# A state-space scan with a gated feed-forward behind it: pair 3 loaded two tokens to a partition and turned by DMA, weights loaded in five groups

## The chip, the cores and the metric

The kernel runs on one core of a Trainium2 chip. The core has five engines with instruction queues of their own: TensorE (PE, with its weight loads PEld) multiplies matrices into PSUM, VectorE (DVE) and ScalarE (ACT) read PSUM and SBUF, GpSimd (POOL) works on SBUF alone, and SyncE (SP) issues DMAs. ACT and POOL issue DMAs too. A DMA that changes the type on its way (the weights here, from fp32 to bf16) is issued by POOL. All DMAs share sixteen DMA engines. An engine runs its own instructions in order, and waits on semaphores for the others.

The metric is device time in microseconds. Thirteen runs of the kernel before have a median of 126.57 us (125.64 to 130.33). The profiled execution took 126.45 us, of which 124.7 us are the profile's span.

## The reference

There are 4 batches of 768 tokens, 8 heads, 32 channels per head and a state of 16. Part one is a linear recurrence with a decay a per token, written by chunks; part two is a feed-forward with a product of two branches:

```python
    for c in range(nc):
        ...
        L = np.exp(cum[:, :, :, None] - cum[:, :, None, :])
        L = L * causal
        CB = np.einsum('bhin,bhjn->bhij', Cc, Bc)
        y_intra = np.einsum('bhij,bhjd->bhid', CB * L, xc)
        y_inter = np.einsum('bhin,bhnd->bhid', Cc, state) * decay_to_i[:, :, :, None]
        y[:, :, sl] = y_intra + y_inter
        state = decay_full[:, :, None, None] * state + np.sum(Bx, axis=2)
...
    gate = np.maximum(x @ w_gate, 0.0)
    val = x @ w_val
    return (gate * val @ w_out).astype(np.float32)
```

In part two x is y laid out as 3072 tokens by 256 channels, and the hidden width is 1536.

## The kernel before

The tokens are cut into twelve **pairs** of 256 tokens (two chunks of 128); three pairs make a batch, so pairs 0 to 2 are batch 0 and pair 3 is the first of batch 1. For the feed-forward two pairs make a **block** of 512 tokens; there are six blocks. While TensorE runs the feed-forward of one block, the pieces of the scan for the next pairs are put between, in an order written out by hand. `in_order` ties every engine to that order, so a late instruction holds back all that stand behind it on its engine.

For each pair C and B (`bcr`) and x (`xr`) are loaded, C is multiplied by the running decay of each token and B by its inverse (`scale_wide`, `scale_bc`), x is cast to bf16 (`cast_x`), and B and C are brought with the state dimension onto the partitions. `G` or `G_wide` forms C times B in four PSUM banks, one for four of sixteen head slots each; ACT copies and DVE evacuate them to `gs`, with the causal mask applied on the way or by POOL behind (`gmask`, `gevac`). `adds` or `sums` forms B times x, from which the state is carried. `inter` adds the state's share to y in PSUM, `D_wide` or `Dm` the share within the chunk; `yevac` writes y, transposed, to `yT`, which the feed-forward reads.

The pairs come in two layouts. Pairs 0 to 2 (`p < NWIDE`) are loaded with two neighbouring tokens to a partition: a piece of 128 bytes for B and C and of 256 for x, 1024 pieces a load, three loads a pair. Pairs 3 to 11 are loaded one chunk at a time, one token to a partition: pieces of 64 and 128 bytes, six loads a pair, each with 1024 pieces again. Pairs 0 to 3 are turned on TensorE (`turn`: four transposes into PSUM, then `tevac` or `copy_B` and `copy_C`). Pairs 4 to 11 (`p >= FIRST`) are scaled by POOL into one of four cleared tiles `tok` and turned by a DMA that transposes (L306, on SP), into `turned`.

The feed-forward: `gv` computes gate and val for 128 of the 1536 hidden channels and all 512 tokens, `gvh` for 256 tokens (u names the half of the block); ACT takes the Relu into r, DVE multiplies by val from PSUM into h. `fout` multiplies h by `wo` for 128 tokens, twelve matmuls; `foevac` writes out. Five PSUM banks are shared by all of these (`bank`).

The order of loads is set by three queues. SP issues the loads of pairs 0 and 1, then, once a DVE memset in the target has run (L84, behind yT of pair 0), C, B and x of pair 2, the six loads of pair 3, and the six each of pairs 4 and 5. Behind them come two stores, the turning of pair 4, the loads of pair 6, the turning of pair 5, the loads of pair 7. POOL issues the weights: wg and wv for hidden slices 0 to 1, then 2 to 5, once `wfac` is there (the copy to `gate`, L718); slices 6 to 11 behind the scaling and casting of pair 1; wo, in one piece, behind a mask of pair 1 (L193). Behind these POOL scales pair 2, builds masks, casts pair 2's x, clears the `tok` tiles, masks pair 2 and scales pair 3 (L315).

Later on POOL scales pairs 4, 5 and 6 in turn (L301, L331), and only behind pair 6 masks the scores of pair 4 (L513).

Of the kernel before, what the change touches and what calls it, by code (L numbers as in the profile page):

```python
# [29 lines left out]
def kernel(  # L30
# [44 lines left out]
    NWIDE = PPB  # L75
# [3 lines left out]
    def load_bc(p, j, *qs):  # L79
        s = st.setdefault(p, {})  # L80
        if "bcr" not in s:
            s["bcr"] = raw.tile([128, NH, 2, 2, N], FP32, tag="bcr", name="bcr")
            if p == 2:
                nc.vector.memset(s["bcr"][0:1, 0, 1, 0, 0:1], 0.0)  # L84
        n = NH // len(qs)
        for i, q in enumerate(qs):
            hs = slice(i * n, (i + 1) * n)
            q.dma_start(
                out=s["bcr"][:, hs, j].rearrange("p h r n -> p h (r n)"),
                in_=(B, C)[j][0, hs, p * 256:(p + 1) * 256, :].rearrange(  # L90
                    "h (p r) n -> p h (r n)", r=2))

    def load_x(p, *qs):
        xr = raw.tile([128, NH, 2, D], FP32, tag="xr", name="xr")
        n = NH // len(qs)
        for i, q in enumerate(qs):
            hs = slice(i * n, (i + 1) * n)
            q.dma_start(out=xr[:, hs].rearrange("p h r d -> p h (r d)"),  # L98
                        in_=x[0, hs, p * 256:(p + 1) * 256, :].rearrange(
                            "h (p r) d -> p h (r d)", r=2))  # L100
        st.setdefault(p, {})["xr"] = xr
# [84 lines left out]
    def weights(f0, f1):  # L186
        fs = slice(f0 * 128, f1 * 128)
        for w, src in ((wg, moe_w_gate), (wv, moe_w_val)):
            nc.gpsimd.dma_start(
                out=w[:, :, fs], in_=src[:, fs].rearrange("(k p) f -> p k f", k=2))  # L190
# [5 lines left out]

    gate = const.tile([1, 2], FP32)
# [36 lines left out]
    def middle():  # L234
        nc.vector.reciprocal(rmid, cp[:, H - 1:H])
        nc.gpsimd.tensor_scalar_mul(pick[:, 0], pairs[:, 0], rmid)

    scaleBC = glob.tile([128, NB, NC, 2, 8], FP32)

    def decay():  # L240

        d = mm.tile([128, HC, 2, NB, 8], FP32, tag="tp", name="dec")
        for k in range(HC):
            nc.tensor.matmul(
                out=d[:, k].rearrange("p w b h -> p (w b h)"),
                lhsT=cp[:, k * 128:(k + 1) * 128],
                rhs=pick.rearrange("p w h -> p (w h)"),
                start=(k == 0), stop=True, skip_group_check=True)
        st["dec"] = d

    def decay_factors():
        d = st["dec"]
        for w in range(2):
            cs = slice(w * HC, (w + 1) * HC)
            nc.scalar.copy(
                out=scaleBC[:, :, cs, 1, :].rearrange("p b k h -> p k b h"), in_=d[:, :, w])
# [11 lines left out]

    def scale_wide(p, j, eng):
        s = st[p]  # L270
        if "bs" not in s:
            s["bs"] = bs = att.tile([128, 4, 128], BF16, tag="bs", name="bs")
            s["tin"] = [[bs[:, 2 * j + r] for r in range(2)] for j in range(2)]
        src = s["bcr"].rearrange("s (t q) j r n -> s j r t q n", t=2)[:, j]
        f = wfac[:, j, :, :, p]
        for t in range(2):
            eng.tensor_tensor(
                out=s["bs"][:, 2 * j:2 * j + 2].rearrange(
                    "s k (q t n) -> s k t q n", q=4, t=2)[:, :, t],
                in0=src[:, :, t],  # L280
                in1=f[:, :, 4 * t:4 * t + 4].to_broadcast([128, 2, 4, N]),
                op=ALU.mult)

    FIRST = 4
    NTOK = 4
    tok = [glob.tile([128, 6, 128], BF16, name="tok%d" % i) for i in range(NTOK)]

    def scale_bc(p, eng):
        b, c0 = p // PPB, 2 * (p % PPB)
        s = st[p]
        if p >= FIRST:
            bs = tok[p % NTOK]
            src = s["bcr"].rearrange("s i j (t q) n -> s j i t q n", t=2)
            f = scaleBC[:, b, c0:c0 + 2].rearrange("s c j h -> s j c h")
            dst = bs.rearrange("s (j i) (q t n) -> s t j i q n", i=2, q=4, t=2)
            for t in range(2):
                for j in range(2):  # L300
                    eng.tensor_tensor(  # L301
                        out=dst[:, t, j * (1 + t)], in0=src[:, j, :, t],
                        in1=f[:, j, :, 4 * t:4 * t + 4].to_broadcast([128, 2, 4, N]),
                        op=ALU.mult)
            turned = att.tile([128, 6, 128], BF16, tag="turned", name="turned", bufs=4)
            nc.sync.dma_start_transpose(out=turned, in_=bs.rearrange("s k c -> s (k c)"))  # L306
            s["B"] = [bs[:, i] for i in range(2)]
            s["BT"] = turned[:, 0:2]
            s["CT"] = turned[:, 2:6].rearrange("s (t i) m -> s t i m", t=2)
            return  # L310
        bs = att.tile([128, 4, 128], BF16, tag="bs", name="bs")
        src = s["bcr"].rearrange("s i j (t q) n -> s (i j) t q n", t=2)
        f = scaleBC[:, b, c0:c0 + 2].rearrange("s c j h -> s (c j) h")
        for t in range(2):
            eng.tensor_tensor(  # L315
                out=bs.rearrange("s k (q t n) -> s k t q n", q=4, t=2)[:, :, t],
                in0=src[:, :, t],
                in1=f[:, :, 4 * t:4 * t + 4].to_broadcast([128, 4, 4, N]),
                op=ALU.mult)
        s["tin"] = [[bs[:, 2 * i + j] for i in range(2)] for j in range(2)]  # L320
        s["B"] = s["tin"][0]
# [67 lines left out]
    def G_wide(p):  # L389
        s = st[p]  # L390
        g = [bank("g%d" % q, (128, 2, 2, 128)) for q in range(4)]
        for r in range(2):
            for i in range(2):
                for q in range(4):
                    rows = slice(32 * q, 32 * q + 32)
                    nc.tensor.matmul(
                        out=g[q][64 * i:64 * i + 64, r],
                        lhsT=s["BT"][rows, r, 64 * i:64 * i + 64], rhs=s["CT"][rows, :, i],
                        start=(r == 0), stop=True, tile_position=(32 * q, 64 * i),
                        skip_group_check=True)  # L400
# [4 lines left out]
    def gmask(p, q, eng, psum=False):  # L405
        s = st[p]
        d = s["gw"][:, q]
        m = wmask.unsqueeze(2).to_broadcast([128, 2, 2, 128])
# [6 lines left out]
    def y_wide(p):  # L415
        s = st[p]
        if "yw" not in s:
            s["yw"] = [mm.tile([128, 512], FP32, tag=t, name=t) for t in ("y", "Aps")]
# [58 lines left out]

    def D_wide(p, qs=(0, 1, 2, 3)):
# [13 lines left out]
    def yevac_wide(p, *engs):  # L492
        s = st[p]
        for i, eng in enumerate(engs):
            dst = yT[:, :, p * 256 + i * 128:p * 256 + (i + 1) * 128]
            (eng.copy if eng is nc.scalar else eng.tensor_copy)(
                out=dst, in_=s["yw"][i][:, 0:256].rearrange("s (t m) -> s t m", t=2))
# [40 lines left out]
    def sums(p):  # L538
# [7 lines left out]
        if c < NC - 2:  # L546
            parts += [(1, s, 0), (1, s, 1)]
        for n, (k, u, i) in enumerate(parts):
            xs = u["x"][i].rearrange("s (t q d) -> s q t d", t=2, q=4)
            for q in range(4):  # L550
                rows = slice(32 * q, 32 * q + 32)
                nc.tensor.matmul(  # L552
                    out=acc["A"][rows, k].rearrange("s (t d) -> s t d", t=2),
                    lhsT=u["B"][i][:, rows], rhs=xs[:, q],
                    start=(c == 0 and n == 0), stop=True, tile_position=(0, 32 * q),
                    skip_group_check=True)
# [92 lines left out]
    def fout(b, ts):  # L649
        if ts % 2 == 0 or b == NBLK - 1:  # L650
# [11 lines left out]
        for f in range(NF):  # L662
# [55 lines left out]
    nc.gpsimd.tensor_copy(gate[:, 0:1], wfac[0:1, 1, 0, 0, 0:1])  # L718
    weights(0, 2)
    weights(2, 6)  # L720
# [11 lines left out]
    cast_x(1, P_)  # L732
# [9 lines left out]
    gcopy(0, 1)  # L742
# [3 lines left out]
    gmask(0, 1, V)  # L746
# [9 lines left out]
    load(2)  # L756
    load(3)
    carry(0, 1)
    weights(6, NF)
    tevac(1, V, A_)  # L760
    pass_on(0, 1)
# [5 lines left out]
    G_wide(1)  # L767
    adds(1)
    decay()
# [7 lines left out]
    gmask(1, 1, P_)  # L777
    weights_out(0, NF)
    gmask(1, 0, V)
    late = [gvh(0, f, 0, True) for f in (1, 2, 3)]  # L780
# [9 lines left out]
    load(4)  # L790
    load(5)
# [7 lines left out]
    for t in range(2):  # L799
        nc.gpsimd.tensor_scalar_mul(smask[:, t], bd, tmask[:, t:t + 1])  # L800
    halves(0, 1, 0, 1, 2, 3, 4, 5)
    gv(0, 6)
    carry(1, 1)
    gv(0, 7)
    pass_on(1, 1)
# [5 lines left out]
    gv(0, 10)  # L811
    gv(0, 11)
    copy_C(2, 1)
    cast_x(2, P_)
    for t in tok:
        nc.gpsimd.memset(t, 0.0)
# [3 lines left out]
    adds(2)  # L820
# [3 lines left out]
    gmask(2, 0, P_)  # L824
    inverse(1, 2)
    gmask(2, 3, V, True)
    gmask(2, 1, V)
    carry(2, 0)
    pass_on(2, 0)
    scale_bc(3, P_)  # L830
    cast_x(3, P_)
    fout(0, 1)
    foevac(0, 1)
# [5 lines left out]
    turn(3)  # L839
    tevac(3, A_, V)  # L840
    fout(0, 3)
    foevac(0, 3)
    G(3)
    sums(3)
    gevac(3)
    states(3)
    halves(1, 0, 0, 1, 2, 3)
    inverse(2, 4)
    inter(3, 1)
    Dm(3)  # L850
    yevac(3, A_)
    halves(1, 0, 4, 5)

    for b in range(1, NBLK):
# [25 lines left out]
        for f in range(n, NF):  # L880
            gv(b, f)
            if b == 1 and at("scale P", 99, 6):
                scale(P, nc.gpsimd, nc.gpsimd)
                load(P + 2)
            if at("scale Q", 9, 6, 4):
# [65 lines left out]
```

## Time and profile before

| what | us |
|---|---|
| median of 13 runs | 126.57 |
| profiled execution | 126.45 |
| its span | 124.7 |
| TensorE busy | 118.1 |
| DVE, ACT, POOL busy | 87.1, 77.0, 47.3 |
| weights and wo, POOL's issue to landing | 4.6 to 10.8 |
| narrow loads of B, C, x on SP, median to landing | 3.7, 3.4, 3.6 |
| a turning DMA on SP, to landing | 3.2 |

In a list of waits a line names the engine and line that idled, what ended the idling, and the sum, the count and the longest, in us. In a timeline a line has the start from the beginning of the span, the duration, the engine (a q behind it is its queue, which issues DMAs), the line, the operation, the tiles as out<-in, the shape and the count of merged instructions; in brackets is the idle time before it and what ended it. The busy table gives busy time, share of the span and number of instructions for each engine.

### The profile page before, as it was taken

To read this page: it belongs to the slowest core of one execution; us is meant where nothing else is said; L and a number is where in the kernel's file an instruction comes from. 1 tells how busy PE (TensorE), PEld (TensorE's weight loads), DVE (VectorE), ACT (ScalarE), POOL (GpSimd) and SP (SyncE) were. 2 spreads that over 40 slices of the span, in tenths; PEclk is the share of its full clock that TensorE was granted. 3 is DMA by queue.
4 is the path that set the end of the run, shared out by engine and by line. 5 is a ranking of instruction groups with operands and counts; after the bars stand their busy time and mean duration, and the time that the engine had idled before them with its cause. 6 is when DMAs were issued, how large, how long until landed. Compare 5 with 4: busy or idle time off the path is not lost.

```text
span 124.7 us, 3580 instructions
## 1 busy us (share of the span) xinstructions
PE 118.1 (95%) x1362; PEld 82.3 (66%) x1368; DVE 87.1 (70%) x192; ACT 77.0 (62%) x169; POOL 47.3 (38%) x106
## 2 busy tenths in 40 slices
PE   6988899997999999999999999999999999999990
PEld 6855585375777468884467874577864677854790
DVE  3795989655499757698853987764997855687510
ACT  0467688844588634787734786726786545876410
POOL 6589622789282309360423810621800033000000
PEclk9999999999999999999999999999999999999999
DMA  3999999977998998699799189991340002200022
GB/s 58 217 173 205 152 222 204 124 89 95 117 119 174 157 120 123 80 251 132 86 114 158 40 180 119 115 158 33 129 104 5 0 0 84 85 4 0 0 84 84
DMA packets 78704, 13.71 MB, mean 110 GB/s; under 512 B 72304, under 2 KB 78688, under 8 KB 78688
## 3 DMA queue, kind: packets, MB, share of 16 engines
q1 hardware_dynamic: 72448, 10.42, 54.2%
q0 software_dynamic: 3184, 2.36, 12.7%
q10 hardware_dynamic: 3056, 0.72, 2.7%
q8 instruction: 10, 0.16, 0.5%
q14 instruction: 6, 0.05, 0.1%
HBM read 11.13 MB, written 3.15 MB: 114 GB/s over the span
## 4 chain that ended last, share of the span: by engine, by line
PE 79%; SPq 11%; DMA 2%; issue 2%; POOL 1%; DVE 1%; ACT 1%; DVEq 0%
PE o L663 22%; PE gv L636 16%; PE val L621 14%; PE gate L618 12%; SPq L116 6%; PE w L180 4%; SPq L117 3%; PE y L593 3%; PE g L505 2%; DMA bcr<-in_C_dram 2%; SPq L98 2%; PE y L582 2%; PE o L657 1%; POOL bs L315 1%; PE A_ps L552 1%
## 5 line engine op out<-in xcount | busy, mean ns | idle before, releaser
L625 DVE TENSOR_TENSOR h<-r,val 128x512 bf16<-128x512 bf16 x44 | 30.3, 688 | 8.2 <-ACT r L624 7.8
L663 PE MATMUL o<-wo,h 128*128 128x256 bf16 x276 | 32.8, 273 | 0.4 <-DMA wo<-in_moe_w_out_dram 0.4
L624 ACT ACTIVATE r<-gate 128x512 bf16<-128x512 f32 x44 | 26.3, 597 | 9.7 <-PE gate L618 9.3
L663 PEld LDWEIGHTS <-h 128*128 128x128 bf16 x276 | 26.0, 98 | 5.5 <-issue 1.5
L621 PE MATMUL val<-yT,wv 128*128 128x512 bf16 x88 | 26.2, 379 | 0.3
L618 PE MATMUL gate<-yT,wg 128*128 128x512 bf16 x82 | 24.9, 379 | 0.0
L642 DVE TENSOR_TENSOR h<-r,gv 128x256 bf16<-128x256 bf16 x56 | 22.5, 418 | 2.5 <-ACT r L639 1.6
L639 ACT ACTIVATE r<-gv 128x256 bf16<-128x256 f32 x56 | 21.4, 384 | 2.3 <-PE gv L636 0.2
L636 PE MATMUL gv<-yT,wv 128*128 128x256 bf16 x112 | 21.4, 273 | 0.5 <-DMA wv<-in_moe_w_val_dram 0.5
L636 PE MATMUL gv<-yT,wg 128*128 128x256 bf16 x112 | 21.5, 273 | 0.2 <-DVE bcr L84 0.2
L530 DVE TENSOR_TENSOR gs<-g,maskUT 128x512 bf16<-128x512 f32 x18 | 11.6, 686 | 12.1 <-issue 5.6
L513 POOL TENSOR_SCALAR_AFFINE_SELECT gs<-gs 128x512 bf16<-128x512 bf16 (+1 forms) x18 | 8.9, 520 | 28.3 <-ACT gs L524 28.3
L301 POOL TENSOR_TENSOR tok<-bcr,scaleBC 128x128 bf16<-128x128 f32 x32 | 12.0, 402 | 20.1 <-DMA bcr<-in_B_dram 19.7
L621 PEld LDWEIGHTS <-wv 128*128 128x128 bf16 x88 | 8.6, 98 | 10.4 <-DMA wv<-in_moe_w_val_dram 0.2
L618 PEld LDWEIGHTS <-wg 128*128 128x128 bf16 x88 | 8.6, 98 | 8.9
L636 PEld LDWEIGHTS <-wv 128*128 128x128 bf16 x112 | 10.9, 98 | 2.0 <-DMA wv<-in_moe_w_val_dram 0.7
L636 PEld LDWEIGHTS <-wg 128*128 128x128 bf16 x112 | 10.2, 98 | 2.2 <-issue 0.4
L524 ACT CAST gs<-g 128x512 bf16<-128x512 f32 x9 | 5.3, 587 | 6.7 <-PE g L505 6.7
L606 ACT CAST yT<-y 128x512 bf16<-128x512 f32 x9 | 5.3, 585 | 5.4 <-PE y L593 2.7
L180 PE MATMUL w<-warm 128*128 128x128 bf16 x49 | 5.9, 296 | 1.1 <-DVE tmask L154 1.1
L180 PEld LDWEIGHTS <-warm 128*128 128x128 bf16 x58 | 5.3, 132 | 1.7 <-DVE tmask L154 1.1
L564 DVE TENSOR_TENSOR Sm<-A_ps,smask 128x256 bf16<-128x256 f32 x15 | 5.7, 416 | 0.0
(115 smaller groups left out, 111.1 us busy)
## 6 DMA issues: line engine op xcount, KB each, us to landing
xr<-in_x_dram SPq DMA_DIRECT2D x19, 128.0 KB, 3.6
out_dram<-ob SPq DMA_DIRECT2D x3, 512.0 KB, 3.3
bcr<-in_C_dram SPq DMA_DIRECT2D x19, 64.0 KB, 3.4
bcr<-in_B_dram SPq DMA_DIRECT2D x19, 64.0 KB, 3.7
out_dram<-ob SPq DMA_DIRECT2D x4, 256.0 KB, 3.0
wo<-in_moe_w_out_dram POOLq DMA_DIRECT2D x1, 768.0 KB, 10.8
xr<-in_x_dram SPq DMA_DIRECT2D x2, 256.0 KB, 9.3
wg<-in_moe_w_gate_dram POOLq DMA_DIRECT2D x1, 384.0 KB, 6.4
```

Source lines behind the costliest of these rows:

```text
L180: nc.tensor.matmul(out=w, lhsT=warm, rhs=rhs, start=True, stop=True)
L301: eng.tensor_tensor(out=dst[:, t, j * (1 + t)], in0=src[:, j, :, t], in1=f[:, j, :, 4 * t:4 * t + 4].to_broadcast([128, 2, 4, N]), op=ALU. ...
L513: nc.gpsimd.affine_select(out=dst, in_=dst, pattern=[[0, n], [1, 128]], compare_op=ALU.is_ge, fill=0.0, base=0, channel_multiplier=-1)
L530: nc.vector.tensor_tensor(out=d[:, q], in0=g[q], in1=m, op=ALU.mult)
L618: nc.tensor.matmul(out=g, lhsT=wg[:, k, fs], rhs=yT[:, k, tk], start=(k == 0), stop=(k == 1))
L621: nc.tensor.matmul(out=v, lhsT=wv[:, k, fs], rhs=yT[:, k, tk], start=(k == 0), stop=(k == 1))
L624: nc.scalar.activation(r, g, AF.Relu)
L625: nc.vector.tensor_tensor(out=fst[b][:, f], in0=r, in1=v, op=ALU.mult)
L636: nc.tensor.matmul(out=gv_[:, j], lhsT=w[:, k, fs], rhs=yT[:, k, tk], start=(k == 0), stop=(k == 1), skip_group_check=True)
L639: nc.scalar.activation(r, gv_[:, 0], AF.Relu)
L642: nc.vector.tensor_tensor(out=fst[b][:, f, u * 256:(u + 1) * 256], in0=r, in1=gv_[:, 1], op=ALU.mult)
L663: nc.tensor.matmul(out=o[:, ts % 2], lhsT=fst[b][:, f, ts * 128:(ts + 1) * 128], rhs=wo[:, f], start=(f == 0), stop=(f == NF - 1), skip_gr ...
```

## The change

Pair 3 now has the layout of two tokens to a partition, and is scaled into `tok` and turned by DMA. Its decay factors `fac3` come from four more fp32 matmuls in `decay`, which stands ahead of the sums of pair 1 now. Its G, D and y use the wide routines with a second mask (`wmask3`), its sums and those of pair 4 read the wide layout, its state's share is added by `inter_full`, and y leaves by ACT and DVE in halves.

The loads change places: of pair 2 only C and B are loaded early; its x waits for a DVE memset that stands behind h of slice 7, and pair 3's three loads follow it. The loads of pairs 4 and 5 stand behind pair 3's turning DMA on SP. The weights come as slices 0-1, 2-3, 4-5, 6-7 and 8-11, wo in two halves; their first DMA waits for a DVE memset in `wg`, and the last pieces are issued one after the other ahead of pair 2's scaling. Casting pair 1's x, the `pick` product and one mask of pair 1 go from POOL to DVE; the clearing of `tok` goes ahead of casting pair 2's x; pair 2's sums go behind `fout(0, 1)`.

```diff
-    NWIDE = PPB
+    NWIDE = PPB + 1
...
     def load_x(p, *qs):
         xr = raw.tile([128, NH, 2, D], FP32, tag="xr", name="xr")
+        if p == 2:
+            nc.vector.memset(xr[0:1, 0, 0, 0:1], 0.0)
...
-    def weights(f0, f1):
+    def weights(f0, f1, which=(0, 1)):
...
-        nc.gpsimd.tensor_scalar_mul(pick[:, 0], pairs[:, 0], rmid)
+        nc.vector.tensor_scalar_mul(pick[:, 0], pairs[:, 0], rmid)
...
+        for r in range(2):
+            for i in range(2):
+                nc.tensor.matmul(
+                    out=d3[64 * i:64 * i + 64, r], lhsT=cp[:, i * 128 + r:i * 128 + 128:2],
+                    rhs=pick[:, 0, NH:2 * NH], start=(r == 0), stop=True,
+                    tile_position=(0, 64 * i), skip_group_check=True)
...
+    def turn_dma(p):
+        s = st[p]
+        bs = tok[p % NTOK]
+        s["turned"] = turned = att.tile([128, 6, 128], BF16, tag="turned", name="turned", bufs=4)
+        nc.sync.dma_start_transpose(out=turned, in_=bs.rearrange("s k c -> s (k c)"))
...
+    def inter_full(p, i):
+        s = st[p]
+        Sm = S.pop(2 * p + i)
+        y = s["yw"][i][:, 0:256].rearrange("s (t m) -> s t m", t=2)
+        for t in range(2):
+            nc.tensor.matmul(
+                out=y[:, t], lhsT=Sm[:, t],
+                rhs=s["turned"][:, 2 + 2 * t:4 + 2 * t, 64 * i:64 * i + 64],
+                start=not s["begun"][i] and t == 0, stop=False, skip_group_check=True)
...
-    nc.gpsimd.tensor_copy(gate[:, 0:1], wfac[0:1, 1, 0, 0, 0:1])
+    nc.vector.memset(wg[0:1, 0, 0:1], 0.0)
     weights(0, 2)
-    weights(2, 6)
+    weights(2, 4)
+    weights(4, 6, (0,))
...
-    cast_x(1, P_)
+    weights(4, 6, (1,))
...
-    gcopy(0, 1)
     gmask(0, 3, V, True)
     keep_warm(4, st[0]["gw"][:, 3, 0, 0])
     gmask(0, 0, V)
-    gmask(0, 1, V)
+    gmask(0, 1, V, True)
...
-    load(2)
-    load(3)
+    load_bc(2, 1, nc.sync)
+    load_bc(2, 0, nc.sync)
     carry(0, 1)
-    weights(6, NF)
+    weights(6, 8)
+    weights(8, NF)
+    weights_out(0, NF // 2)
+    weights_out(NF // 2, NF)
     tevac(1, V, A_)
+    cast_x(1, V)
...
+    decay()
     adds(1)
-    decay()
...
-    gmask(1, 1, P_)
-    weights_out(0, NF)
     gmask(1, 0, V)
+    gmask(1, 1, V)
...
     decay_factors()
-    load(4)
-    load(5)
...
+    for t in tok:
+        nc.gpsimd.memset(t, 0.0)
+    wmask3 = const.tile([128, 2, 128], BF16)
...
     gv(0, 7)
+    load_x(2, nc.sync)
+    load(3)
+    nc.vector.reciprocal(fac3[:, 0], fac3[:, 1])
...
     cast_x(2, P_)
-    for t in tok:
-        nc.gpsimd.memset(t, 0.0)
+    scale_wide(3, 1, P_)
+    scale_wide(3, 0, P_)
+    turn_dma(3)
+    load(4)
+    load(5)
+    cast_x(3, P_)
...
-    turn(3)
-    tevac(3, A_, V)
     fout(0, 3)
     foevac(0, 3)
-    G(3)
+    G_wide(3)
     sums(3)
-    gevac(3)
+    gcopy(3, 0)
+    gmask(3, 2, V, True)
+    gcopy(3, 1)
+    gmask(3, 0, P_)
+    gmask(3, 3, V, True)
     states(3)
-    halves(1, 0, 0, 1, 2, 3)
-    inverse(2, 4)
-    inter(3, 1)
-    Dm(3)
-    yevac(3, A_)
-    halves(1, 0, 4, 5)
+    gmask(3, 1, V)
+    halves(1, 0, 0, 1, 2, 3, 4)
+    y_wide(3)
+    inter_full(3, 1)
+    D_wide(3)
+    yevac_wide(3, A_, V)
+    halves(1, 0, 5)
```

## The prediction

> **What bounds the kernel now.** I read the page's busy table first, then TensorE's list of waits, then the timelines of the SP queue, GpSimd (POOL) and VectorE (DVE) between 14 and 50 us.
>
> ```profile
> PE 118.1 (95%) x1362; PEld 82.3 (66%) x1368; DVE 87.1 (70%) x192; ACT 77.0 (62%) x169; POOL 47.3 (38%) x106
> ...
> PE w L180 <- DVE tmask L154: 1.1, 1, 1.1
> PE tp L345 <- POOL bs L315: 0.7, 1, 0.7
> PE gv L636 <- DMA wv<-in_moe_w_val_dram: 0.5, 1, 0.5
> PE Aps L472 <- ACT Sw L460: 0.4, 1, 0.4
> PE o L663 <- DMA wo<-in_moe_w_out_dram: 0.4, 1, 0.4
> ```
>
> TensorE is busy for 118.1 of 124.7 us. Of its idle time 1.1 us lies before the first matmul and 2.8 us behind the last one; a change here has only the last four waits (2.0 us) to win. The other thing to see is hidden: TensorE is only just on time at 49.6 us, and what it waits for there hangs on the SP queue.
>
> ```profile
> 27.40 0.58 SPq L116 DMA_DIRECT2D bcr<-in_B_dram  x1
> ...
> 36.55 0.76 SPq L117 DMA_DIRECT2D xr<-in_x_dram  x1
> 37.41 2.05 SPq L703 DMA_DIRECT2D out_dram<-ob  x2
> 39.55 1.35 SPq L306 DMA_TRANSPOSE turned<-tok  x1
> ...
> 44.57 0.58 SPq L117 DMA_DIRECT2D xr<-in_x_dram  x1
> ```
>
> ```profile
> 46.68 1.62 POOL L301 TENSOR_TENSOR tok<-bcr,scaleBC 128x128 bf16<-128x128 f32 x4 [4.98 <-DMA bcr<-in_B_dram]
> 48.24 0.61 POOL L331 CAST xb<-xr 128x512 bf16<-128x512 f32 x1
> 48.81 0.99 POOL L513 TENSOR_SCALAR_AFFINE_SELECT gs<-gs 128x512 bf16<-128x512 bf16 x2
> ```
>
> ```profile
> 49.61 0.53 PE L593 MATMUL y<-gs,xb 128*32 128x128 bf16 x16
> ```
>
> SP issues the loads of pairs 4, 5 and 6 back to back from 27.40 to 45.15. POOL scales pair 6 when its B has landed (46.6, after 4.98 us of idling), casts its x, and only then masks pair 4's scores (48.81 to 49.80). Pair 4's sixteen y matmuls need that mask: they take 0.53 us here, 0.34 in pair 3, and the second half starts at 49.86, just behind the mask. So this chain has no slack: what delays SP's loads by d delays TensorE by about d, and TensorE being early gains nothing.
>
> **The change part by part.**
>
> *Start, 0 to 16 us.* A DVE memset (0.06, as L84) replaces POOL's copy (0.30) as what holds the weights back. POOL then issues five weight DMAs instead of four before it scales pair 1: 4.5 + 0.93 + 4 x 0.72 = 8.3, against 8.21 before: 0.1, with no one waiting. Casting pair 1's x (0.60) goes to DVE, into an idle of 0.84 us there; the pick product (0.37 on POOL) goes into the 0.52 us before L496. Without the second score copy on ACT, Sw starts at 8.9 instead of 9.24, so most of the 0.44 us wait at L472 goes; next late is DVE's mask from PSUM (8.68 + 0.61 + 0.65 = 9.95), which leaves 0.15 us. The decay matmuls get four more fp32 ones; the nearest row, the factors at L209 (eight passes, 0.56), prices them at 0.5, with 0.1 (their eight columns alone) as the other end. That fills the hole of the wv wait (0.45), which goes, because wv for f = 2 and 3 now has 512 KB ahead of and with it instead of 768: wg(2,6), at that place now, landed at 11.5, wv at 14.1. Pair 1's mask moves from POOL (1.15) to DVE (0.41 to 0.69), in time for D at 15.2. Together -0.15.
>
> *Weights.* Splitting adds five POOL issues of about 0.72 (seven weight DMAs become twelve): 10.2 + 7 x 0.75 = 15.5, where the wo issue ended at 15.39. Nothing waits for that, since pair 2's C landed at 16.5. wo now competes with no load of x2 or pair 3, so the 0.36 us wait goes. The Trainium skill ("DMA: Bandwidth & Descriptors", Rules for kernel authors and Anatomy of one DMA) speaks against splitting: at least 1 MiB per transfer, and some 2 us fixed per DMA. By that page five more would be +10 us, an estimate, if each stood alone. The first four weight DMAs, issued 0.72 apart, landed at 9.66, 10.25, 11.49 and 14.12: they overlap, and I charge the issue alone.
>
> *Pair 3's transposes leave TensorE.* The 0.69 us wait for bs L315 and the four transposes (0.23) go. Added: 16 G matmuls for 8 (0.35 for 0.33), 32 D for 16 (0.35 for 0.34), four more sums in pairs 3 and 4 each (0.06): +0.15, which falls behind pair 3's G and into the wait found below. So TensorE could reach pair 3's G at 32.89 - 0.15 - 0.36 - 0.92 = 31.45.
>
> *Pair 3's turning.* x of pair 2 now waits for a DVE memset behind h of f = 7 (21.92 before, 21.8 now), and C, B, x of pair 3 are queued behind it on SP. The four landings follow from rows: issue to first landing as unhindered loads have it (a 64 KB half of C with the same 128-byte pieces: 2.6 us, its data 0.5), then 1.5 us for a wide x (x of pair 1: 9.62 - 8.13) and 0.85 for each wide B or C (1024 packets of 128 bytes at the trace's 13 ns on sixteen engines; C of pair 1 took 1.06 with other loads beside it). x2 lands at 25.4, C3 26.3, B3 27.1. POOL then has four scalings of 0.39; the last two need B3: 27.1 + 0.1 + 0.8 = 28.0. But POOL also has its own path:
>
> ```profile
> 21.08 0.77 POOL L277 TENSOR_TENSOR bs<-bcr,wfac 128x128 bf16<-128x128 f32 x2 [3.64 <-DMA bcr<-in_B_dram]
> ...
> 23.25 1.19 POOL L800 TENSOR_SCALAR smask<-bd,tmask 128x128 bf16<-128x128 bf16 x2
> 25.36 0.61 POOL L328 CAST xb<-xr 128x512 bf16<-128x512 f32 x1 [0.91 <-DMA xr<-in_x_dram]
> 25.90 2.77 POOL L816 MEMSET tok<- 128x768 bf16 x4
> ```
>
> The 2.77 us of memsets now stand ahead of the cast, with a mask copy (not in the trace; between 0.2, a memset of half its size, and 1.15, the mask product of twice its size; I take 0.45). From B2's landing L: 0.8 + 2.6 + 2.8 + 0.45 + 0.6 + 1.6 = L + 8.9. With L at 21.0 as now the turning DMA is issued at 29.9. Of the sixteen landing marks of that DMA fourteen are in by 16.7; the last, slow under the weights, is 21.0. I take L = 19.7, between, nearer the late end, as C and B still meet the weights. Issue: **28.6**, bounds 27.6 and 29.9. The turned tile lands 3.2 us later, at 31.8: TensorE waits 0.35 there. Pair 2's cast x, ready by L + 7.3 = 27.0, is needed at 27.8, since its sums moved behind fout(0, 1).
>
> *VectorE behind G.* Half of pair 3's y now leaves by DVE, queued behind five h of half a block:
>
> ```profile
> 33.45 1.29 DVE L530 TENSOR_TENSOR gs<-g,maskUT 128x512 bf16<-128x512 f32 x2 [0.67 <-PE g L505]
> ...
> 34.99 0.75 DVE L564 TENSOR_TENSOR Sm<-A_ps,smask 128x256 bf16<-128x256 f32 x2
> 35.65 1.41 DVE L642 TENSOR_TENSOR h<-r,gv 128x256 bf16<-128x256 bf16 x4
> ```
>
> From G: 0.35 + 0.17 + 1.29 + 0.75 + 0.41 + 5 x 0.35 + 0.42 = 5.1 us. With G at 31.8 TensorE takes up the other half of block 1 at 36.9, where it did so at 36.89 before: nearly all that was won is given back there, and with G at 31.45 0.3 us is left.
>
> *SP's queue.* The loads of pairs 4 and 5 stand behind the turning DMA: first issue 28.6 + 1.4 = 30.0, against 27.40, 2.6 late. Their number and pieces are unchanged, and the DMA engines were busy for 0.90, 0.90, 0.95 and 0.89 of the time between 30 and 50 us, so they can catch up about 8% of 17.75 = 1.4 us, less if the queue's stops return. At 28.6: d = **+1.2**; bounds +0.2 (27.6, all caught up) and +3.5 (29.9, 0.4 caught up).
>
> **Sum.** Won up to pair 3's G: 0.15 + 0.36 + 0.92 less the 0.35 wait; DVE takes it back; pair 4's mask comes 1.2 us late and sets the end, since nothing behind 50 us changes. 126.45 + 1.2 = 127.65 for the profiled execution, 0.12 below the median: 127.7.
>
> **The rivals.**
> *Faster.* The four removed waits count. For it: each is a row. It decides when the turning DMA is issued by about 26.9, or the DMA engines run full; then d is under zero. The DVE queue leaves 0.3, and without that limit 1.4: 126.2 to 125.1. Against it: x2 cannot be issued before h of f = 7, and three landings follow.
> *POOL late.* B2 lands at 21.0 again: issue at 29.9, G at 33.1, block 1's other half 1.3 late, d = 2.5 to 3.5: 129.0 to 130.0. For it: the 3.64 us idle above. Against: SP sends nothing behind B2 until 21.8.
> *The swap is even.* d of 0.2 and 0.3 won elsewhere: 126.2 to 126.9.
>
> **How the numbers follow.** A run's time tells about 0.3% (0.38 us). Main case, +0.4 to +2.0: 0.47, its own range 127.0 to 128.5. POOL late: 0.17. Even: 0.15. Faster by over 0.38: 0.21, as the sum of long chains may be wrong by a microsecond. Slower: 0.64. The range 126.0 to 129.2 leaves out about 1 in 10 at each end.
>
> **What would show it.** Right: the turning DMA of pair 3 issued at 28 to 29; no wait at L345 for bs, nor for wo; POOL idle until pair 6's B lands at 47 to 48.5, and y of pair 4 behind its mask near 51. Wrong: that DMA before 27, or pair 6's mask chain ending before 49.8; then TensorE's removed waits set the time.

## The result and the profile after

The changed kernel takes 128.3 us in the median (11 runs, 127.61 to 129.93), the kernel before beside it 126.46 (48 runs). The ratio is 1.0155, 95% interval [1.0122, 1.0188]: slower by about 1.8 us. The first profiled execution of it took only 126.84 us (span 125.1), 1.5 below the median, so it isn't the usual one; the changed kernel was therefore profiled a second time, without any edit (the run `again`, 127.62 us, span 125.9), and the two profiles are read side by side.

The busy table of the changed kernel, first profile (busy us, share of the span, instructions):

```profile
PE 118.4 (95%) x1398; PEld 82.9 (66%) x1404; DVE 89.1 (71%) x199; ACT 76.4 (61%) x168; POOL 48.1 (38%) x108
```

TensorE is busy for 118.4 us, 0.3 more than before (118.2 in `again`), so the loss isn't work. Its list of waits in the same profile (line, what ended the wait; sum, count and longest in us):

```profile
PE gv L678 <- DVE yT L532: 1.3, 1, 1.3
PE w L184 <- DVE tmask L158: 1.1, 1, 1.1
PE y L518 <- DVE gs L428: 0.2, 1, 0.2
```

The same list of `again`, nearer to the usual execution:

```profile
PE y L635 <- POOL gs L548: 1.4, 1, 1.4
PE gv L678 <- DVE yT L532: 1.3, 1, 1.3
PE w L184 <- DVE tmask L158: 1.1, 1, 1.1
```

The waits for bs (0.7), wv (0.5) and wo (0.4) are gone, as the change meant. One of 1.3 for yT has come in both, and in `again` another of 1.4 for the mask of pair 4. The first of the two, on the timelines of DVE and TensorE (start, duration; in brackets the idle time before it) in the first profile:

```profile
32.15 1.29 DVE L428 TENSOR_TENSOR gs<-g,wmask 128x512 bf16<-128x512 f32 x2 [1.40 <-PE g L413]
33.35 0.75 DVE L606 TENSOR_TENSOR Sm<-A_ps,smask 128x256 bf16<-128x256 f32 x2
34.02 0.53 DVE L428 TENSOR_TENSOR gs<-gs,wmask 128x512 bf16<-128x512 bf16 x1
34.46 1.73 DVE L684 TENSOR_TENSOR h<-r,gv 128x256 bf16<-128x256 bf16 x5
36.12 0.43 DVE L532 CAST yT<-y 128x256 bf16<-128x256 f32 x1
...
31.54 0.42 PE L413 MATMUL g<-turned 32*64 32x256 bf16 x16
...
36.61 0.28 PE L678 MATMUL gv<-yT,wg 128*128 128x256 bf16 x1 [1.34 <-DVE yT L532]
```

TensorE begins pair 3's G at 31.54, goes on with what is left of the first half of block 1, and cannot take up the other half until DVE has gone through two masks, two Sm, another mask, five h and at last the half of yT. From G to the other half of block 1 that is 5.07 us here, and 5.07 again in the second profile (30.89 to 35.96).

The second wait, on POOL's and TensorE's timelines of `again`:

```profile
46.36 0.40 POOL L333 TENSOR_TENSOR tok<-bcr,scaleBC 128x128 bf16<-128x128 f32 x1 [4.86 <-DMA bcr<-in_B_dram]
47.06 1.12 POOL L333 TENSOR_TENSOR tok<-bcr,scaleBC 128x128 bf16<-128x128 f32 x3 [0.29 <-DMA bcr<-in_C_dram]
49.31 0.61 POOL L348 CAST xb<-xr 128x512 bf16<-128x512 f32 x1 [1.14 <-PE y L624]
49.88 1.00 POOL L548 TENSOR_SCALAR_AFFINE_SELECT gs<-gs 128x512 bf16<-128x512 bf16 x2
...
50.57 0.65 PE L635 MATMUL y<-gs,xb 128*32 128x128 bf16 x16 [1.35 <-POOL gs L548]
```

Pair 6's B comes at 46.2, as in the kernel before (46.5), but the cast of its x waits 1.14 us. The bracket names a TensorE instruction; what landed just before the cast, at 49.16, was x of pair 6 (47.62 in the kernel before). So a releaser in brackets is to be checked against the landings.

Where TensorE stands, from its timeline in four kernels (the last is an experiment told of below):

| start of, us | before | changed, first | changed, `again` | `turn5_first` |
|---|---|---|---|---|
| pair 3's G | 32.89 | 31.54 | 30.89 | 30.73 |
| block 1, other half | 36.90 | 36.61 | 35.96 | 35.78 |
| block 1, first whole gate | 39.52 | 39.57 | 38.92 | 38.73 |
| block 2, first whole gate | 56.04 | 56.09 | 57.11 | 55.26 |
| end of the last matmul | 121.87 | 122.15 | 122.92 | 122.00 |

In `again` TensorE is 2.0 us early at pair 3's G; 1.1 of that is gone at the other half of block 1 and 0.3 more at the whole gate; at block 2 it is 1.07 late and stays so (1.05 at the end). The loss lies between 39 and 57 us. The two kernels take 16.52 us for that stretch in the profile before and in the changed kernel's first, and 18.19 in `again`: 1.35 of the difference is the wait for the mask, and 0.24 is y behind it, which takes 0.65 against 0.41 in the first profile. Less the lead of 0.60 at the whole gate this gives the 1.05 us by which `again` ends its last matmul later; the medians differ by 1.8, and no profile shows what makes the other 0.7 or so.

### The profile page after: what moved, and what is told of

It reads as the page before. It is cut to its first block, busy times and chain, and to the rows that moved or that the text cites. A ratio compares the mean times of both kernels' runs of the same rounds, so it can differ in the third digit from the quotient of the medians.

```text
span 125.1 us, 3656 instructions
## 1 busy us (share of the span) xinstructions
PE 118.4 (95%) x1398; PEld 82.9 (66%) x1404; DVE 89.1 (71%) x199; ACT 76.4 (61%) x168; POOL 48.1 (38%) x108
## 3 DMA queue, kind: packets, MB, share of 16 engines
q1 hardware_dynamic: 70128, 10.61, 53.7%
## 4 chain that ended last, share of the span: by engine, by line
PE 88%; DVE 6%; DMA 3%; issue 1%; ACT 0%; DVEq 0%
PE o L705 23%; PE gv L678 18%; PE val L663 16%; PE gate L660 14%; PE w L184 4%; DVE gs L428 3%; DMA turned<-tok 3%; PE g L540 2%; PE y L635 2%; PE g L413 1%; DVE h L684 1%; PE y L624 1%; PE o L699 1%; PE y L518 1%; PE A_ps L593 1%
## 5 line engine op out<-in xcount | busy, mean ns | idle before, releaser
L666 ACT ACTIVATE r<-gate 128x512 bf16<-128x512 f32 x44 | 26.3, 597 | 9.7 <-PE gate L660 9.3
L548 POOL TENSOR_SCALAR_AFFINE_SELECT gs<-gs 128x512 bf16<-128x512 bf16 (+1 forms) x16 | 7.9, 520 | 28.5 <-ACT gs L559 28.5
L565 DVE TENSOR_TENSOR gs<-g,maskUT 128x512 bf16<-128x512 f32 x16 | 10.3, 687 | 11.6 <-issue 7.2
L559 ACT CAST gs<-g 128x512 bf16<-128x512 f32 x8 | 4.7, 588 | 6.8 <-PE g L540 6.7
L648 ACT CAST yT<-y 128x512 bf16<-128x512 f32 x8 | 4.7, 585 | 5.1 <-PE y L635 2.5
L428 DVE TENSOR_TENSOR gs<-g,wmask 128x512 bf16<-128x512 f32 x9 | 5.9, 681 | 2.7 <-PE g L413 2.7
```

The costliest lines, as they stand in the source:

```text
L428: eng.tensor_tensor(out=d, in0=s["gp"][q] if psum else d, in1=m, op=ALU.mult)
L565: nc.vector.tensor_tensor(out=d[:, q], in0=g[q], in1=m, op=ALU.mult)
L666: nc.scalar.activation(r, g, AF.Relu)
```

## The experiments

All ratios are to the kernel before, measured beside the run; where only six runs were made the interval is wide.

### The changed kernel once more

> The changed kernel once more, for a second profile: the first one took 126.84 us, 1.5 us below the median of 128.3, so it does not show the usual execution. Load theory: in the usual execution pair 3's turning DMA is issued 1 to 2 us later than the 27.73 us of the first profile, because pair 2's B lands later than 17.3 us or x2, C3, B3 land later, and TensorE's wait for VectorE's y of pair 3 moves with it (36.61 becomes 37.6 to 38.6). Rival, VectorE queue alone: everything as in the first profile, the wait of 1.34 us included, and the rest is scatter of the measurement. Time 128.3 by both.

Measured: 127.75 us, ratio 1.0135 [1.0079, 1.0191]; its profile is read above. The turning of pair 3 was issued at 27.27, the loads of pair 4 from 28.64 on.

### Are the weights' groups what lets pair 3 be turned in time?

```
-    weights(2, 4)
-    weights(4, 6, (0,))
+    weights(2, 6)
...
-    weights(4, 6, (1,))
...
-    weights(6, 8)
-    weights(8, NF)
-    weights_out(0, NF // 2)
-    weights_out(NF // 2, NF)
+    weights(6, NF)
+    weights_out(0, NF)
```

> The changed kernel with the weights in the groups of before (slices 0-1, 2-5, 6-11, wo whole). Packets of 512 bytes took 60 ns and of 1536 bytes 140, so the five groups cost the DMA engines about 1.3 us more. If that makes pair 2's B and the loads behind late, this one is 0.5 to 1 us faster; if the groups matter only for the wait for wv (0.45 in the profile of before), it is the same within 0.4 us, or up to 0.4 slower.

Measured: 133.11 us, ratio 1.050 [1.0433, 1.0567]. POOL's and SP's timelines:

```profile
20.47 0.78 POOL L317 TENSOR_TENSOR bs<-bcr,wfac 128x128 bf16<-128x128 f32 x2 [8.30 <-DMA bcr<-in_C_dram]
23.00 0.77 POOL L317 TENSOR_TENSOR bs<-bcr,wfac 128x128 bf16<-128x128 f32 x2 [1.75 <-DMA bcr<-in_B_dram]
...
31.82 1.33 SPq L294 DMA_TRANSPOSE turned<-tok  x1
```

C and B of pair 2 share the DMA engines with weights that are cut less finely: they land at 20.33 and 22.93, against 15.04 and 16.29 in `again`. POOL stands idle for 8.30 and 1.75 us, and pair 3 is turned 4.55 us later. This is the rival called POOL late, with its own formula: landing of B plus 8.9 is 31.83, and the turning was issued at 31.82. In the changed kernel it doesn't happen, because the groups prevent it; they are worth some 5 us there (133.11 against 127.75).

### Do the groups alone help the kernel before?

```
-    weights(2, 6)
+    weights(2, 4)
+    weights(4, 6, (0,))
...
     cast_x(1, P_)
+    weights(4, 6, (1,))
...
-    weights(6, NF)
+    weights(6, 8)
+    weights(8, NF)
...
-    weights_out(0, NF)
+    weights_out(0, NF // 2)
+    weights_out(NF // 2, NF)
```

> The kernel before with the weights in five groups and wo in two halves, and nothing else. The groups alone were worth about 5 us inside the changed kernel (133.1 with the old groups). If that is because packets of 512 bytes let pair 2's C and B through, they land here by 18 as well (21.0 before) and the waits for wv (0.45) and wo (0.36) shrink: 0.3 to 0.9 us faster than before. If it came from the place where POOL issues them, or from x2 being out of the way, it is the same within 0.4 us.

Measured: 127.0 us, ratio 1.008 [1.0042, 1.0118]: slower, against the expectation. C and B of pair 2 landed at 16.23 and 19.09 (16.52 and 21.02 before), and the waits for wv and wo are gone, but others came. DVE's and POOL's timelines of this run, then of the kernel before:

```profile
8.67 2.55 DVE L410 TENSOR_TENSOR gs<-gs,wmask 128x512 bf16<-128x512 bf16 x2
...
8.52 1.53 POOL L278 TENSOR_TENSOR bs<-bcr,wfac 128x128 bf16<-128x128 f32 x4
```

```profile
8.59 1.22 DVE L409 TENSOR_TENSOR gs<-gs,wmask 128x512 bf16<-128x512 bf16 x2
...
8.21 1.88 POOL L277 TENSOR_TENSOR bs<-bcr,wfac 128x128 bf16<-128x128 f32 x4 [0.42 <-DMA bcr<-in_C_dram]
```

With an issue more ahead of it on POOL, the scaling of pair 1 runs from 8.52 to 10.05 in this run, just over these two masks, and they take 1.33 us longer; TensorE waits 0.8 for them and the loads of pair 2, behind a memset on DVE, start 1.5 late (12.40 against 10.88). Near 50 us it waits 0.7 for pair 4's mask. The profiled execution took 127.78 us, and TensorE's granted clock was at half from 10.6 to 14.0 in it, so a part of its lateness can be that. The Trainium skill, "SBUF — State Buffer" (Who interferes with whom), says that a DVE instruction with two SBUF inputs and a GpSimd instruction that reads SBUF exclude each other. The 2.55 us agree with it, though in the kernel before the two overlap as well and DVE takes 1.22, while the scaling takes 1.88 instead of 1.53. That this is what makes the kernel slower isn't shown.

### The start, and the half of yT on DVE

The first puts the removed score copy back on ACT:

```
     gcopy(0, 0)
+    gcopy(0, 1)
...
-    gmask(0, 1, V, True)
+    gmask(0, 1, V)
```

> Head slot 1 of pair 0 goes back to ScalarE's copy and a mask in SBUF. In the first profile the first half-block matmul stands at 11.30 against 10.98 before: 0.32 lost in the first 12 us, with waits for VectorE's masks of 0.14 and 0.20. Theory of the start: these 0.3 us come back in the time. Load theory: nothing, since the wait for VectorE at 36.6 or pair 3's turning, both late for other reasons, absorbs them; the half-block matmul may stand 0 to 0.3 earlier.

Measured: 128.51 us, ratio 1.0166 [1.0114, 1.0218], the same as the changed kernel. In its profile the first matmul of a half block stands at 10.84 us, between the 11.30 and 10.49 of the changed kernel's two profiles: whatever the start wins or loses doesn't show at the end.

The second takes half of pair 3's y off DVE's queue:

```
-    yevac_wide(3, A_, V)
+    yevac_wide(3, A_, A_)
```

> Both halves of pair 3's y leave by ScalarE, so that none is queued behind the five h on VectorE. VectorE-queue theory: TensorE's wait of 1.34 us at the second half of block 1 shrinks to about 0.4 (ScalarE ends the second half near 35.9 instead of 36.55), so 0.7 to 0.9 us are won, if the chain of pair 6's loads and pair 4's mask has that much slack (in the first profile the mask ended at 49.17 and was needed at 49.80: 0.6). Load theory: 0 to 0.6 won, since the mask chain of pair 4 takes over.

Measured: 127.79 us, ratio 1.0135 [1.0087, 1.0183], exactly as `again`. TensorE's list of waits:

```profile
PE y L635 <- POOL gs L548: 1.8, 1, 1.8
PE w L184 <- DVE tmask L158: 1.1, 1, 1.1
PE y L624 <- DMA turned<-tok: 0.9, 1, 0.9
PE gv L678 <- ACT yT L532: 0.7, 1, 0.7
```

The wait for yT is halved, and the turned tile of pair 4 and the mask take the gain: what TensorE wins at 36 us is worth nothing while the chain near 50 us is late.

### Is it the mask's place behind pair 6's x?

In `mask_first` POOL scales pair 6 only after it has masked pair 4:

```
-            if at("scale next P", 11, 11, 9) and P + 2 < NPAIR:
+            if at("scale next P", 11, 99, 9) and P + 2 < NPAIR:
...
             if b == 1:
                 states(P)
+                scale(P + 2, nc.gpsimd, nc.gpsimd)
```

> GpSimd masks pair 4's scores before it scales pair 6, instead of behind it. Load theory: in the usual execution of the changed kernel (its second profile) the y matmuls of pair 4 wait 1.35 us at 50.57 for that mask, which stands behind pair 6's x (landed at 49.16). With the mask first it ends near 48.4 and the wait goes: 1.0 to 1.35 us faster than the changed kernel, 126.4 to 126.8, unless pair 5's turned tile (landed 49.89, needed by then at 49.8) or pair 6's sums wait instead. Rival (the wait is only moved time, and a wait of VectorE or of the banks holds the same end): within 0.4 us of the changed kernel.

Measured: 127.32 us, ratio 1.0119 [1.0064, 1.0173], not clearly below the changed kernel. TensorE's timeline:

```profile
49.11 0.41 PE L635 MATMUL y<-gs,xb 128*32 128x128 bf16 x16
49.35 0.23 PE L593 MATMUL A_ps<-xb,tok 128*32 128x64 bf16 x8
50.39 0.40 PE L540 MATMUL g<-turned 32*128 32x256 bf16 x8 [0.81 <-DMA turned<-tok]
```

The wait for the mask is gone, and the turned tile of pair 5, which landed at 50.34, is late next, for 0.81 us. So the mask alone isn't the cause: x of pair 6 and the turning behind it are late together.

### Why are that load and that turning late?

SP sent the load at about the same time as before (44.91 in `again`, 44.57 before). What differs is a fetch of instructions, a packet of 16 KB on a queue of its own, which takes 0.9 to 1.5 us in this stretch. I take it for TensorE's: the profile before has 10 such packets for 2730 matmuls and weight loads, the changed kernel's two have 11 for 2802. It ran at 49.28 in the kernel before, and at 46.35 in `again`, just beside the two. The DMA's own view from 44 to 50 us, in 40 slices of 0.15 us (busy share in tenths, then GB/s), first of the kernel before:

```profile
DMA  7999999998996799789999998487889899660047
GB/s 115 147 167 166 164 148 105 91 90 86 95 119 77 105 128 149 108 132 179 242 242 243 188 278 176 64 86 76 79 82 98 80 124 112 60 125 1 0 71 119
```

The same of `again`:

```profile
DMA  9999747979989999667799999991100008900684
GB/s 178 189 172 142 114 66 92 96 69 104 103 82 100 115 95 181 100 95 117 117 161 213 226 248 212 136 46 9 10 9 11 15 19 176 233 17 0 65 79 39
```

And of `mask_first`:

```profile
DMA  9994379997599999999999999000010000499999
GB/s 191 183 150 73 53 82 98 113 119 71 59 91 105 118 118 149 198 149 157 171 231 242 320 130 10 0 0 0 0 7 9 10 10 10 89 275 156 145 145 140
```

From 47.9 to 48.9 in `again`, and from 47.6 to 49.1 in `mask_first`, nearly nothing moves; then all resume. The 9 to 10 GB/s are what one engine carries (a packet of 128 bytes in 13 ns). An engine's share of x is 64 such packets, 0.83 us, about the length of the low stretch in `again`. I read this as one engine, put back by the fetch, that still carries its share of x while the other fifteen stand still, so that x's load is only complete at the end.

A load has sixteen landing marks, as many as there are DMA engines, and they bear out the first half. Where no turning stands behind a load, one mark is late. B of pair 6 in `turn5_first` (fetch at 46.80) has fifteen marks by 47.48 and the last at 48.79; in `turn5_first_act` (fetch at 47.11) it is fifteen by 47.47 and the last at 49.13. In the kernel before (fetch at 49.28) the load that is hit is C of pair 7, with fifteen by 49.89 and the last at 51.58, and TensorE doesn't wait for it. With the turning behind, most marks are late together: in `again` one mark of x came at 47.57 and fifteen from 49.07 to 49.16.

How long the later half of x of pair 6 took from its issue to landing:

| | no fetch before it landed | fetch beside it |
|---|---|---|
| turning of pair 5 issued right behind it | 3.04 (before), 3.05 (changed, first), 3.53 (`before_groups`) | 4.26 (`again`), 4.37 (`copy_back`), 3.69 (`y3_on_act`), 4.73 (`mask_first`), 4.84, 4.93 and 4.52 (`before_more_pe`, `fewer_pe`, `fewer_pe_again`, below), 3.20 (`weights_as_before`) |
| turning ahead of the load instead | 3.69 (`before_reordered`) | 3.36, 3.49 (`turn5_first`, `turn5_first_act`) |

With the fetch and the turning both beside it, x took 4.26 to 4.93 us in six profiles of eight; in these the fetch began 1.44 to 3.08 us after the load's issue. In the other two it began 0.86 and 0.68 after it, and their 3.69 and 3.20 are no longer than a load without a fetch can take. With the turning ahead x isn't late, but B of the same half is: 4.06 and 4.37 with a fetch, against 3.47 in `before_reordered`. So the fetch makes a load late without the turning's help. That the transposing DMA makes the other engines wait for the last one is my reading of these rows; no run shows the rule itself. The three profiles of 127.6 us and more in which nothing is edited near 50 us (`again`, `copy_back`, `y3_on_act`) all have the fetch at 46.35 to 47.00 and a wait of 1.2 to 1.8 for the mask.

Two kernels were to move the fetch by TensorE's instruction count. The first adds a second `D_wide(2)` to the kernel before:

```
     D_wide(2)
+    D_wide(2)
```

> The kernel before with pair 2's share within its chunks added twice, so that pair 2's y holds it double: 64 more TensorE instructions, 0.35 us of TensorE time at 30 us. Instruction-fetch theory: the fetch at 49.3 moves to about 46, beside pair 6's loads; x lands at 48.5 or later instead of 47.6, the mask of pair 4 is late, and the time rises by 0.8 to 1.8 us. Rival, the loads alone: 0 to 0.35 us more, since the 0.69 us wait for pair 3's scaling directly behind hides it.

Measured: 126.32 us, ratio 1.0028 [0.9987, 1.007]. The time did not rise by the expected 0.8 us or more; it fits the rival. The profile (127.44 us) does have what the theory said, the fetch at 46.55 and x of pair 6 at 49.05, and TensorE waits:

```profile
PE y L593 <- POOL gs L513: 1.6, 1, 1.6
PE w L180 <- DVE tmask L154: 1.1, 1, 1.1
```

This is the changed kernel's wait, in the kernel before with 64 instructions more. Of its twelve runs eight took 125.3 to 126.9 us and four 127.4 to 128.2, and the profile is of the latter: most executions may not have the wait.

The other leaves the same instructions out of the changed kernel:

```
-    D_wide(2)
```

> The 32 matmuls and 32 weight loads of pair 2's share within its chunks are left out, so pair 2's y lacks that share. Instruction-fetch theory: TensorE's instructions come in pieces of 16 KB (256 instructions) through the same DMA engines. In the changed kernel one piece is fetched at 46.4 to 47.6, beside pair 6's x, which then lands at 49.1 to 49.5; before it was fetched at 49.3 and x landed at 47.6. 64 instructions fewer put that fetch some 3 us later (about 49.5): x lands by 48.0, the wait for pair 4's mask is 0.4 us or less, time 126.4 to 127.0. Rival, the loads themselves are late (turning DMA of pair 3 late, queue full): x still lands near 49, and the time falls by no more than 0.35 us.

Measured: 126.66 us, ratio 1.0054 [1.0012, 1.0095], some 1 us below the changed kernel, as expected, though up to 0.6 of that can be the work left out. The profiled execution took 131.14 us, with TensorE's granted clock at half from 53.7 to 57.1, and isn't the usual one. Up to 53 us it still speaks against the theory: the fetch came at 49.04, as late as was said, but the load went out later too (45.96 against 44.91 in `again`), so the two met, x landed at 50.90, and TensorE waited 2.63 us for the mask. The kernel was run a second time:

> The kernel of fewer_pe once more, for a profile of a usual execution: without the step that adds pair 2's own positions into its y (64 instructions of TensorE fewer; the output lacks that share). If the fetch theory holds, the fetch of instructions falls at 48.5 to 49.5 instead of 46 to 47.5, x of pair 6 lands before 48 and no wait for the mask stands near 50; time 126.7, about 1 below the changed kernel. If the gain came from elsewhere (0.6 less work on TensorE alone), x of pair 6 lands at 49 or later all the same and the mask's wait of 1.0 to 1.4 stands.

Measured: 126.54 us, ratio 1.0021 [0.9987, 1.0055]. The profile (127.65 us; nine of the twelve runs took 125.7 to 126.8) has the fetch at 47.06, not at 48.5 or later, x of pair 6 at 49.20 and 1.58 us of waiting for the mask. So the fetch did not move as I had said, and by what was said beforehand this profile speaks for the rival, that the gain is the work left out. It is of one of the three slower executions, though; whether the fetch falls elsewhere in the faster ones, no profile shows. The time fits both.

### Turning pair 5 ahead of pair 6's loads

In `turn5_first` the edit of `mask_first` stays, and on SP's queue the turning of pair 5, which could go at 41, no longer stands behind six loads:

```
                 scale(P, nc.gpsimd, nc.gpsimd)
-                load(P + 2)
                 inverse(2, 4)
...
                 scale(Q, nc.gpsimd, nc.gpsimd)
                 if b == 1:
+                    load(P + 2)
                     load(P + 3)
```

> The run mask_first, with one instruction more moved: on SP's queue the turning of pair 5 stands ahead of the six loads of pair 6 instead of behind them (pair 5 is scaled by about 41, but its turning was issued at 45.4, behind those loads). Theory (what is left of the loss in the usual execution, once the mask is out of the way, is pair 5's turning, late only because it is issued among pair 6's loads and lands beside an instruction fetch): turning issued at 41 to 42, landed by 45.5, its wait of 0.81 gone and nothing in its place; x of pair 6 lands at 49.5 to 50.5, which nobody waits for any more; time 126.5, the wait of 1.3 for yT is left. Rival (the stretch is limited by what the queue carries, and something else comes late in its place, at first the turning of pair 6 or pair 4): 127.3 as before, with a new wait of 0.5 to 1 between 43 and 70.

Measured: 126.59 us, ratio 1.0012 [0.9982, 1.0042]. The loss is gone. SP's and TensorE's timelines:

```profile
39.80 2.84 SPq L294 DMA_TRANSPOSE turned<-tok  x2
42.69 0.57 SPq L120 DMA_DIRECT2D bcr<-in_B_dram  x1
...
49.37 0.40 PE L540 MATMUL g<-turned 32*128 32x256 bf16 x8
49.70 1.48 PE L705 MATMUL o<-wo,h 128*128 128x256 bf16 x12
...
68.12 0.40 PE L540 MATMUL g<-turned 32*128 32x256 bf16 x8 [0.85 <-DMA turned<-tok]
```

Pair 5's turned tile landed at 44.51, and nothing waits at 50 us though the fetch fell at 46.80. TensorE reaches block 2 at 55.26, 0.78 ahead of the kernel before. The rival holds for the rest: pair 7's turning, issued at 64.94, landed at 68.07, about when it did before (67.94), so TensorE, which is early now, waits 0.85 for it at 68.12, and that eats the lead.

With both halves of pair 3's y on ACT besides:

> As turn5_first, and both halves of pair 3's y go through ACT, as in y3_on_act. Theory (the two waits behind yT, of 0.86 for pair 4's turning and of 1.8 for the mask, were what took back y3_on_act's gain; the second of them is away now): 0.4 to 0.7 less than turn5_first, 125.8 to 126.1, the wait for yT 0.66 instead of 1.34; if pair 4's turning lands by 43.6 the whole 0.7. Rival (pair 4's turning is late by as much as TensorE comes early): the same time as turn5_first, with a wait of 0.6 to 0.9 near 44.5 for turned of pair 4.

Measured: 126.49 us, ratio 1.0017 [0.9979, 1.0055]. In its profile the wait for yT is 0.7 instead of 1.3 and the one at pair 7's G 0.3 instead of 0.9, and the span 124.5 instead of 125.0; the medians don't tell the two kernels apart.

The same two edits on the kernel before, as a control:

> The kernel before, with both edits of turn5_first (POOL scales pair 6 only behind pair 4's mask; pair 5's turning stands ahead of pair 6's loads). If these edits repair only what the change made late: within 0.3% of the kernel before, 126.0 to 126.7, since there no wait stands at pair 4's mask or pair 5's turning in its profile. Rival (the same lateness falls in many executions of the kernel before too, those of 127.4 to 130, which its one profile does not show): 0.3 to 0.7 below it, and the spread of its runs shrinks.

Measured: 126.35 us, ratio 0.9994 [0.996, 1.0028]: no difference. So they mend what the change made late, and aren't a gain in themselves. The turning moved alone, without the mask, was not run. None of the kernels tried beats the kernel before.

## Why the prediction was right, and where its terms were off

The forecast was 127.7 us and slower, as the likeliest case, at the mask of pair 4 behind pair 6's x. The kernel takes 128.3, inside the range and inside the main case's own range, and `again` loses its time where the prediction said. (The sum is rounded short: the median of 126.57 plus 1.2 is 127.8.) Step by step:

- *Start.* Predicted -0.15. In the two profiles block 0's first whole gate starts 0.04 later and 0.77 earlier than before: single executions differ by more than the term, and `copy_back` shows that it doesn't reach the end.
- *Weights.* The wait for wo went, and the last weight issue ended at 15.50, as worked out (15.5). The rule set against it, batches of at least 1 MiB and some 2 us per DMA (the Trainium skill, "DMA: Bandwidth & Descriptors", Rules for kernel authors and Anatomy of one DMA), would have charged +10 us by the prediction's estimate; here the coarser groups cost 5% more instead. I priced the groups at their issues only and missed that they let pair 2's B land 6.6 us earlier in this kernel.
- *Pair 3's turning.* Landing of B, taken as 19.7, was mis-sized: 17.30 and 16.29. So POOL's own path was never the later one; x, C and B of the two wide pairs were (25.50, 26.00 and 26.48 against 25.4, 26.3 and 27.1), and the turning went at 27.73 and 27.27, not at 28.6. The lower bound of 27.6 was nearest, for which the prediction shows no working: its path through SP's loads ended at 28.0. The wait of 0.35 at G did not come; in return TensorE got there at 31.54 and 30.89, where 31.45 was worked out.
- *VectorE behind G.* 5.1 us predicted, 5.07 measured twice. The other half of block 1 began at 36.61 and 35.96 instead of 36.9, since G was earlier. That DVE takes most of the gain back was right.
- *SP's queue.* This is the step that failed. The loads of pairs 4 and 5 went 1.2 to 1.7 us later, and I let them catch up 1.4 of 2.6; they caught up all of it (pair 6's B landed at 46.20 and 45.91, before at 46.52). From this step alone the case called even would have followed. x of pair 6 was late all the same, by 1.54 us in `again`, for a reason that no step had: a fetch of instructions in the middle of its load, as far as the profiles show it.
- *The sum.* Pair 4's mask ended 1.08 us later in `again` (50.88 against 49.80), where +1.2 was predicted, and nothing changed behind block 2. That POOL scales pair 6 before it masks pair 4 carries the lateness on, was right; that the mask alone sets the end, was not: with the mask moved, pair 5's turning took its place (0.81), and with that moved as well the loss is undone. The place was right; that the size came out is luck, since the delay that was worked out, SP's late first issue, was caught up in full and another took its place.

Of what would show it, the waits at L345 and for wo did go, POOL idled until 46.1 to 46.4 (47 to 48.5 was said), the turning DMA was early (27.3 to 27.7, not 28 to 29), and y of pair 4 came at 50.57 behind its mask in `again`, at 49.80 without a wait in the first profile. The rival called faster, of removed waits that count, found none of its gain: 2.0 us at pair 3's G were there and didn't last.

Open is how often the fetch falls beside pair 6's loads in the executions of each kernel, since only single ones were profiled, why the other DMA engines stand still beside a turning, what brings the 1 us in `fewer_pe`, and what makes the some 0.7 of the 1.8 us that `again` doesn't have.

## What to carry to other kernels

A wait removed from TensorE is worth only what the next queue lets through: follow the early engine to the next instruction that another engine's queue holds, here 5.07 us of DVE's work and then POOL's order of scale, cast and mask. On a queue that runs in order, what a near consumer needs (a mask, a turning) belongs ahead of what is loaded or scaled for later, above all where a late load can hold it. When two executions of one kernel differ by over 1%, profile a second one before you explain the first.

## What the runs showed that was not expected

- A fetch of 16 KB of instructions, 0.9 to 1.5 us long near 50 us, puts a load beside it back on one of its sixteen landing marks: in three profiles fifteen came in time and the last 1.3 to 1.7 us behind them, and the load took 4.1 to 4.4 us. With a transposing DMA behind the load nearly nothing moved for 1.0 to 1.5 us, and a load of x took 4.3 to 4.9 us in six profiles of eight; without a fetch it took 3.0 to 3.7. The Trainium skill, "Runtime: NRT & Kernel Launch" (Instruction fetch mechanics), has the same 16 KB blocks and calls their cost mostly hidden; for the engine that fetches that holds (no wait in TensorE's lists is put down to a fetch), for the loads beside it these profiles show 1 us and more.
- With 64 instructions of TensorE more, 2% of them, that fetch came 2.7 us earlier in the kernel before, and a wait of 1.56 us stood far from the added work (one profile of each kernel).
- Loads of 128 KB behind coarse weight transfers took 9.5 and 11.7 us to land (C and B of pair 2 in `weights_as_before`), behind the finer ones 4.6 and 5.5.
